# Last stage of a fused kernel: blocks read back in halves, a turn moved into the next tile, five weight loads held back

## The chip, the cores and the metric

The kernel runs on one core of a Trainium2 chip. The metric is the device time of one execution in microseconds, the median of three runs. The core's engines work side by side and wait for each other by semaphores: TensorE (PE, matmuls, with its weight loads as PEld), VectorE (DVE), ScalarE (ACT), GpSimd (POOL) and SyncE (SP), which here issues every DMA.

## The reference, cut to what matters

```
attn = softmax(scale * q_c @ k_c.T) @ v_c        # chunks of 64
x    = rmsnorm(attn) * rms_g
h    = silu(x @ w_gate) * (x @ w_val)            # 4608 x 1536
x2   = h @ w_out                                 # 4608 x 512
u    = x2 @ w_in                                 # 4608 x 2048
g    = u * cos(u)
out  = g @ w_out2                                # 4608 x 512
```

The last stage is the last line: 4608 tokens, 2048 inputs, 512 outputs, in f32. Each f32 operand is split into a high and a low part (`F32R`), and three matmuls stand for one.

## The kernel before

The kernel has four stages one after the other: attention with gate, value and silu; the product with `w_out`; the product with `w_in` and the cosine; and the last product, here the **last stage**. The last three multiply matrices in a Strassen-Winograd form, with seven products of half blocks in the place of eight. The last stage is the one the change is in.

The third stage writes g to DRAM (`gd`, three pieces of 1536 tokens). The last stage walks over NB = 6 tiles `s` of T = 768 tokens, in each over the seven products `j` in the order `PRODUCTS` = 1, 7, 6, 2, 5, 4, 3, and in each product over four groups `g` of 512 inputs. One step (s, j, g) is called a product here: 12 matmuls of 384 columns, `mm3` at L259. A tile has 28 of them.

For each tile and group, `fetch4` reads a block of g back as one SBUF tile `rawg` (128 partitions, 4 x 768 floats, 1.5 MB), in one DMA from the queue of SP (L815; in the first tile in six pieces, L992). The block has four quarters `b(r, c)`. `operand4` makes the operand of a product by `operand`: j = 1 takes b(0, 0) as it is; j = 7 writes b(1,1) - b(0,1) into `tmp` (L232); j = 6 changes b(0,1) and b(0,0) in place (L235, L236); j = 2, 5 and 3 take a quarter as it is; j = 4 subtracts b(0,0) from b(1,0) in place (L243). Then ACT casts the high part (L246) and DVE subtracts it for the low part (L247); both lie in a tile `xo`, of which the pool has five. Up to AHEAD = 5 operands are made ahead of the product that PE is at. `tmp` has one buffer, `rawg` four: one for each group. So a block for the next tile is asked for when the operand of j = 3 has been taken from the old one.

Sums are built up in PSUM. At the end of j = 1, 6 and 5 ACT copies the bank `b1` out (L982); DVE adds banks to it (L986); a finished quarter of the output is turned by DVE (`store`, a STREAM_TRANSPOSE at L974) and leaves by four DMAs (L978). The quarter of j = 3 is turned straight from the bank, after the last product of the tile.

Weights of the last stage lie in 28 places in SBUF, which the weights of the third stage (and the first six operands of the last stage) leave one by one in its last tile. `free` is called with a place as soon as the program has used it for the last time, and loads the next weight into it (L155).

The order of the instructions on each engine is not written out in this stage. A scheduler makes it from the program, the dependencies and its own estimate of times. Each engine then takes its instructions strictly in that order, PE's weight loads apart.

Of the kernel before, what the change touches and what calls it, by code (L numbers as in the profile page):

```python
# [9 lines left out]
F32 = mybir.dt.float32  # L10
# [10 lines left out]
P = 128  # L21
# [13 lines left out]
T = 768  # L35
H = T // 2
# [17 lines left out]

AHEAD = 5
EARLY4 = 6

BEHIND = 2

# [16 lines left out]
def kernel(  # L76
# [57 lines left out]
    last = [("out2", g, PLACE_A[j]) for j in PRODUCTS for g in range(N2 // 4)]  # L134
    wanted += last[:4] + [("op4", n, k) for n in range(EARLY4) for k in range(2)] + last[4:]
    place_of, weight, kept, early = {}, {}, {}, {}

    def free(*tags):
        for tag in tags:
# [77 lines left out]
    def blocks(raw):  # L217

        i = (slice(0, 2), slice(2, 4)), (slice(0, H), slice(H, T))
        return {(r, c): raw[:, i[0][r], i[1][c]] for r in range(2) for c in range(2)}  # L220
# [583 lines left out]
    G4 = N2 // 4  # L804
    raw4, ops4 = {}, {}

    def fetch4(s, g):
        if s < NB:
            t = rw.tile([P, 4, T], F32, tag="raw", name="rawg")
            raw4[s, g] = blocks(t)  # L810
            c = s * T % PIECE
            a = gd[s * T // PIECE][:, g, :, c : c + T]
            if s == 0:
                return t, a
            nc.sync.dma_start(out=t, in_=a)  # L815

    def operand4(s, j, g):
        n = made4[0]
        if n < EARLY4:
            tmp = third_p.tile([P, 2, H], F32, tag="tmp", name="tmp", bufs=1) if j == 7 else None  # L820
            to = [wp.tile([P, 2, H], F32R, tag=place_of["op4", n, k], name="xo") for k in range(2)]
            part = first4[g]
        else:
            tmp = tp.tile([P, 2, H], F32, tag="tmp", name="tmp") if j == 7 else None
            to = parts(xo_p)
            part = raw4[s, g]
        ops4[s, j, g] = operand(j, part, tmp, lambda: to)
        if j == PRODUCTS[-1]:
            fetch4(s + 1, g)

    first4 = {g: {} for g in range(G4)}

# [27 lines left out]
    with ExitStack() as st:  # L860
# [6 lines left out]
        def multiply(acc, s, j, g, first):  # L867
            w = weight["in", g, PLACE_A[j]]
            x = ops3[s, j]
            for p in range(2):  # L870
                mm3(
                    acc[:, p],
                    [(w[:, e, 0, p], w[:, e, 1, p], x[:, 0, e], x[:, 1, e]) for e in range(2)],
                    first,
                )
            if s == NB - 1:
                free(place_of["in", g, PLACE_A[j]])
            if g == G3 - 1 and j != 1:
                ahead3(made3[0] + 1)

# [75 lines left out]
    with ExitStack() as st:  # L956
# [29 lines left out]
            nc.vector.tensor_tensor(to, acc, to, op=ALU.add)  # L986
            return to

        tiles = [fetch4(0, g) for g in range(G4)]
        for g, cut in ((2, slice(H, T)), (3, slice(H, T)), (0, slice(0, T)), (1, slice(0, T)), (2, slice(0, H)), (3, slice(0, H))):  # L990
            t, a = tiles[g]
            nc.sync.dma_start(out=t[:, :, cut], in_=a[:, :, cut])  # L992
        z, xs = {}, {}
        for n, (s, j, g) in enumerate(seq4):
            bank = BANK[j]
            opens = j in (1, 2, 7, 4)
# [12 lines left out]
            product(z[bank], xs[g], g, j, opens and g == 0, slice(0, H))  # L1009
            if n < EARLY4:  # L1010
                free(*(place_of["op4", n, k] for k in range(2)))
            if g < G4 - 1:
                continue
            if j == 1:
                z[1] = saved(z["b1"], "s1")
            elif j == 6:
                z[6] = add(saved(z["b1"], "s6"), z["b3"])
            elif j == 5:
                store(s, 1, 1, add(saved(z["b1"], "s1"), z["b3"]), 0, H)
            elif j == 2:  # L1020
                store(s, 0, 0, add(z[1], z["b2"]), 0, H)
            elif j == 4:
                store(s, 1, 0, add(z[6], z["b4"]), 0, H)
            elif j == 3:
                store(s, 0, 1, z["b1"], 0, H)


# ---- launch: one core; inputs laid out for contiguous loads
# [47 lines left out]
```

## Time and profile before

| | us |
|---|---|
| median of three runs | 1713.21 (1713.1 to 1715.33) |
| the profiled execution | 1714.37 |
| its span, first to last instruction | 1712.2 |
| PE busy | 1663.2 (97%) |
| DVE busy | 1263.4 (74%) |
| ACT busy | 858.7 (50%) |
| mean granted TensorE clock | 0.991 |

PE is the bound nearly everywhere. A wait of PE is a hole in its row of the timeline; what ended it stands in brackets behind it. A group of matmuls in that row goes on as long as PE does not wait. One matmul in a long run takes about 0.174 us, but 0.44 us by itself, because its end is counted from issue to the last result.

### The profile page before, as it was taken

To read this page: it belongs to the slowest core of one execution; us is meant where nothing else is said; L and a number is where in the kernel's file an instruction comes from. 1 tells how busy PE (TensorE), PEld (TensorE's weight loads), DVE (VectorE), ACT (ScalarE), POOL (GpSimd) and SP (SyncE) were. 2 spreads that over 40 slices of the span, in tenths; PEclk is the share of its full clock that TensorE was granted. 3 is DMA by queue.
4 is the path that set the end of the run, shared out by engine and by line. 5 is a ranking of instruction groups with operands and counts; after the bars stand their busy time and mean duration, and the time that the engine had idled before them with its cause. 6 is when DMAs were issued, how large, how long until landed. Compare 5 with 4: busy or idle time off the path is not lost.

```text
span 1712.2 us, 27957 instructions
## 1 busy us (share of the span) xinstructions
PE 1663.2 (97%) x11016; PEld 1542.6 (90%) x11016; DVE 1263.4 (74%) x1831; ACT 858.7 (50%) x1242; POOL 63.0 (4%) x104
## 2 busy tenths in 40 slices
PE   6999999999999999999999999999998999999998
PEld 5988888888888888999999999999998889989988
DVE  7974578877877821777777788888886876876875
ACT  4643344554544421444444588888786433433432
POOL 2321000000000000000000000000000000000000
PEclk9999999999999999999999999999999999999999
DMA  8523587787888747633338733442459645045051
GB/s 324 184 78 111 159 246 222 246 254 238 243 242 236 213 157 254 210 140 138 141 145 271 270 118 135 148 142 104 147 200 354 239 165 185 17 169 182 12 175 38
DMA packets 273699, 310.38 MB, mean 181 GB/s; under 512 B 82592, under 2 KB 217248, under 8 KB 273568
## 3 DMA queue, kind: packets, MB, share of 16 engines
q1 hardware_dynamic: 273568, 308.60, 54.6%
q8 instruction: 87, 1.43, 0.4%
q14 instruction: 44, 0.36, 0.1%
HBM read 183.24 MB, written 125.30 MB: 180 GB/s over the span
## 4 chain that ended last, share of the span: by engine, by line
PE 84%; DMA 6%; DVE 5%; ACT 2%; issue 1%; SPq 0%; POOL 0%; ACTq 0%; DVEq 0%
PE b L259 46%; PE v L259 18%; PE g L259 17%; DMA rawg<-gd 5%; DVE xo L247 1%; PE o L450 1%; ACT xo L246 1%; PE sc L356 1%; PE tr L426 1%; PE pt L394 1%; DVE tmp L232 1%; DMA raw<-in_w_dram 1%; DVE rawg L236 1%; DMA rawx<-x2d 0%; DMA rawx<-gd 0%
## 5 line engine op out<-in xcount | busy, mean ns | idle before, releaser
L259 PE MATMUL b<-xo,w 128*128 128x384 f32 (+1 forms) x3576 | 632.8, 337 | 27.6 <-DVE xo L247 17.4
L259 PEld LDWEIGHTS b<-xo,w 128*128 128x128 f32 x3576 | 622.9, 190 | 37.5 <-DVE xo L247 21.3
L259 PE MATMUL b<-x,w 128*128 128x384 f32 x2016 | 352.1, 335 | 0.4 <-ACT z L886 0.2
L259 PEld LDWEIGHTS b<-x,w 128*128 128x128 f32 x2016 | 349.0, 188 | 3.4 <-ACT z L886 2.7
L259 PE MATMUL v<-xt,w 128*128 128x512 f32 (+1 forms) x1416 | 321.7, 377 | 0.0
L259 PE MATMUL g<-xt,w 128*128 128x512 f32 (+1 forms) x1416 | 314.6, 372 | 0.0
L259 PEld LDWEIGHTS g<-xt,w 128*128 128x128 f32 x1416 | 250.0, 188 | 45.8
L259 PEld LDWEIGHTS v<-xt,w 128*128 128x128 f32 x1416 | 248.3, 190 | 44.9
L246 ACT CAST xo<-rawg 128x768 fp32r<-128x768 f32 x140 | 114.7, 836 | 173.8 <-PE b L259 88.3
L499 ACT ACTIVATE sg<-g 128x512 f32<-128x512 f32 (+1 forms) x118 | 66.0, 560 | 227.2 <-PE g L259 218.4
L247 DVE TENSOR_TENSOR xo<-rawg,xo 128x768 fp32r<-128x768 f32 x140 | 131.1, 952 | 53.8 <-ACT xo L246 53.5
L503 DVE TENSOR_TENSOR h<-sg,v 128x512 f32<-128x512 f32 (+1 forms) x100 | 67.5, 678 | 117.0 <-PE v L259 96.2
L246 ACT CAST xo<-rawh 128x768 fp32r<-128x768 f32 x102 | 81.6, 835 | 95.8 <-DMA rawh<-hd 49.3
L247 DVE TENSOR_TENSOR xo<-rawh,xo 128x768 fp32r<-128x768 f32 x102 | 93.0, 954 | 36.7 <-ACT xo L246 36.7
L903 DVE SCALAR_TENSOR_TENSOR r<-r,u 128x768 f32<-128x768 f32 x72 | 68.6, 953 | 22.5 <-ACT r L902 22.4
L901 ACT ACTIVATE r<-r 128x768 f32<-128x768 f32 x72 | 60.8, 845 | 33.6 <-DVE r L900 33.4
L900 DVE SCALAR_TENSOR_TENSOR r<-r,u 128x768 f32<-128x768 int32 x72 | 68.6, 952 | 10.7 <-ACT r L899 10.7
L891 DVE TENSOR_TENSOR u<-b,z 128x768 f32<-128x768 f32 x72 | 68.5, 952 | 7.6 <-ACT z L886 6.4
L899 ACT CAST r<-u 128x768 int32<-128x768 f32 x72 | 59.7, 829 | 8.4 <-DVE u L891 8.2
L246 ACT CAST xo<-tmp 128x768 fp32r<-128x768 f32 x42 | 35.1, 835 | 53.2 <-DVE tmp L232 53.2
L902 ACT ACTIVATE r<-r 128x768 f32<-128x768 f32 x72 | 61.0, 847 | 1.2
L886 ACT COPY z<-b 128x768 f32<-128x768 f32 x72 | 56.4, 793 | 7.3 <-PE b L259 5.4
(101 smaller groups left out, 1435.0 us busy)
## 6 DMA issues: line engine op xcount, KB each, us to landing
gd<-r SPq DMA_DIRECT2D x96, 384.0 KB, 2.5
rawg<-gd SPq DMA_DIRECT2D x22, 1536.0 KB, 12.4
hd<-h SPq DMA_DIRECT2D x49, 512.0 KB, 4.8
kout<-wout SPq DMA_DIRECT2D x56, 448.0 KB, 4.7
w<-kout SPq DMA_DIRECT2D x49, 512.0 KB, 5.1
rawh<-hd SPq DMA_DIRECT2D x15, 1536.0 KB, 9.1
wraw<-in_w_dram SPq DMA_DIRECT2D x176, 128.0 KB, 3.0
qk<-in_qk_dram SPq DMA_DIRECT2D x36, 512.0 KB, 6.1
```

Source lines behind the costliest of these rows:

```text
L246: nc.scalar.copy(hi, a)
L247: nc.vector.tensor_tensor(lo, a, f32(hi), op=ALU.subtract)
L259: nc.tensor.matmul(acc, a, b, start=first and k == 0 and q == 0, stop=k == n - 1 and q == 2, skip_group_check=True)
L499: nc.scalar.activation(sg, g, AF.Silu)
L503: nc.vector.tensor_tensor(h, silu(acc[0]), acc[1], op=ALU.mult)
L886: nc.scalar.copy(t, acc)
L891: nc.vector.tensor_tensor(t, acc, part, op=ALU.add)
L899: nc.scalar.copy(k, u)
L900: nc.vector.scalar_tensor_tensor(q, k, -1.0, u, op0=ALU.mult, op1=ALU.add)
L901: nc.scalar.activation(q, q, AF.Sin, scale=math.pi)
L902: nc.scalar.activation(q, q, AF.Square, scale=math.sqrt(2 * PI2))
L903: nc.vector.scalar_tensor_tensor(q, q, -PI2, u, op0=ALU.add, op1=ALU.mult)
```

## The change

The block of a tile and group is no longer one tile of four quarter-columns of blocks but two halves, r = 0 with b(0,0) and b(0,1), and r = 1 with b(1,0) and b(1,1). Each half has four buffers of its own, so the space is the same. The half r = 0 of the next tile is asked for when the operand of j = 4 has been made, the half r = 1 when that of j = 3 has: the first half four products earlier than before. In the first tile 14 pieces are read in place of six, those that products 7 and 6 need first.

The turn of the quarter of j = 3 is written behind the second product of the next tile in place of the end of its own. Five of the places that the third stage's last group leaves are kept in a list, and their weights are asked for behind the first tile's blocks.

```diff
+HELD = (2, 7, 5, 4, 3)
...
-    def fetch4(s, g):
+    def fetch4(s, r, g):
         if s < NB:
-            t = rw.tile([P, 4, T], F32, tag="raw", name="rawg")
-            raw4[s, g] = blocks(t)
...
-            nc.sync.dma_start(out=t, in_=a)
+            t = rw.tile([P, 2, T], F32, tag=f"raw{r}", name="rawg")
+            raw4[s, g, r, 0], raw4[s, g, r, 1] = t[:, :, :H], t[:, :, H:]
+            if s:
+                load4(s, r, g, t, 0, T)
+            return t
+
+    def load4(s, r, g, t, lo, hi):
+        c = s * T % PIECE
+        nc.sync.dma_start(out=t[:, :, lo:hi], in_=gd[s * T // PIECE][:, g, 2 * r : 2 * r + 2, c + lo : c + hi])
...
-        if j == PRODUCTS[-1]:
-            fetch4(s + 1, g)
+        if j in (4, 3):
+            fetch4(s + 1, int(j == 3), g)
...
             if s == NB - 1:
-                free(place_of["in", g, PLACE_A[j]])
+                held.append(place_of["in", g, PLACE_A[j]])
+                if not (g == G3 - 1 and j in HELD):
+                    free(held.pop())
...
-        for g, cut in ((2, slice(H, T)), (3, slice(H, T)), (0, slice(0, T)), (1, slice(0, T)), (2, slice(0, H)), (3, slice(0, H))):
-            t, a = tiles[g]
-            nc.sync.dma_start(out=t[:, :, cut], in_=a[:, :, cut])
+        for g, r, lo, hi in (
+            [(g, r, H, T) for g in (2, 3) for r in range(2)]
+            + [(g, r, r * H, T) for g in (0, 1) for r in range(2)]
+            + [(g, 0, 0, H) for g in (2, 3)]
+            + [(g, 1, 0, H) for g in range(G4)]
+        ):
+            load4(0, r, g, both[g][r], lo, hi)
+        free(*held)
+        held.clear()
...
+            if late and g == 1:
+                store(*late.pop())
...
             elif j == 3:
-                store(s, 0, 1, z["b1"], 0, H)
+                late.append((s, 0, 1, z["b1"], 0, H))
```

How the scheduler now puts the instructions is seen at three places. Line numbers have moved by 3 to 7 (L247 is L250, L232 L235, L974 L981, L246 L249, L982 L989, L815 L820, L978 L985).

**DVE where the third tile takes over from the second.** Before, from the turn of j = 4 (`s_13836`) on; `b1_13636` is the second tile's bank, `rawg_13984`, `_14001`, `_14018` and `_14035` are the third tile's blocks:

```order
L974 STREAM_TRANSPOSE o_14050<-s_13836 128x2x12x32
L974 STREAM_TRANSPOSE o_14116<-b1_13636 128x2x12x32
L232 TENSOR_TENSOR tmp_14123<-rawg_13984 128x768
L247 TENSOR_TENSOR xo_14056<-rawg_13984,xo_14056 128x768
L235 TENSOR_TENSOR rawg_13984<-rawg_13984 128x2x384
L236 TENSOR_TENSOR rawg_13984<-rawg_13984 128x2x384
L247 TENSOR_TENSOR xo_14071<-rawg_14001,xo_14071 128x768
L247 TENSOR_TENSOR xo_14086<-rawg_14018,xo_14086 128x768
L247 TENSOR_TENSOR xo_14101<-rawg_14035,xo_14101 128x768
L247 TENSOR_TENSOR xo_14124<-tmp_14123,xo_14124 128x768
```

The same place now; `b1_13650` is the second tile's bank, `rawg_13931`, `_13949`, `_13967` and `_13985` the third tile's halves r = 0, `rawg_14012` the first half r = 1:

```order
L250 TENSOR_TENSOR xo_14084<-rawg_13931,xo_14084 128x768
L981 STREAM_TRANSPOSE o_14078<-s_13856 128x2x12x32
L250 TENSOR_TENSOR xo_14099<-rawg_13949,xo_14099 128x768
L250 TENSOR_TENSOR xo_14114<-rawg_13967,xo_14114 128x768
L250 TENSOR_TENSOR xo_14129<-rawg_13985,xo_14129 128x768
L981 STREAM_TRANSPOSE o_14179<-b1_13650 128x2x12x32
L235 TENSOR_TENSOR tmp_14145<-rawg_14012,rawg_13931 128x768
L238 TENSOR_TENSOR rawg_13931<-rawg_13931 128x2x384
L250 TENSOR_TENSOR xo_14146<-tmp_14145,xo_14146 128x768
L239 TENSOR_TENSOR rawg_13931<-rawg_14012,rawg_13931 128x2x384
```

The four low parts of the new tile's j = 1 stood behind the turn of the old tile's last bank and now stand ahead of it; the turn itself is still ahead of all of j = 7.

**ACT where the second tile takes over from the first.** Before; the `rawg` casts are those of j = 3 and of the new j = 1, `s<-b_13636` copies the second tile's sum of j = 1, the `tmp` casts are j = 7, and the `rawg` casts behind them are j = 6 and 2:

```order
L982 COPY s<-b_13136 128x768
L246 CAST xo<-rawg 128x768 x8
L246 CAST xo<-tmp 128x768 x2
L982 COPY s<-b_13636 128x768
L246 CAST xo<-tmp 128x768 x2
L246 CAST xo<-rawg 128x768 x8
```

Now, where `s<-b_13650` is that copy, and behind it the next boundary, where `s<-b_14144` is the third tile's:

```order
L249 CAST xo<-rawg 128x768 x8
L989 COPY s<-b_13650 128x768
L249 CAST xo<-tmp 128x768 x4
L249 CAST xo<-rawg 128x768 x8
L989 COPY s<-b_13650 128x768
L249 CAST xo<-rawg 128x768 x8
L249 CAST xo<-tmp 128x768 x2
L989 COPY s<-b_14144 128x768
L249 CAST xo<-tmp 128x768 x2
```

At this first boundary the copy now stands ahead of all four casts of j = 7; at the other four it stands between the second and the third, as before.

**SP in the second tile.** Before, with the stores of j = 2 and 5 (`o_13901`, `o_13974`) ahead and those of j = 4 and 3 behind:

```order
L978 DMA out_0_dram<-o_13901 32x12x64 x4
L978 DMA out_0_dram<-o_13974 32x12x64 x4
L815 DMA rawg_13984<-gd1_77 128x4x768
L815 DMA rawg_14001<-gd1_77 128x4x768
L815 DMA rawg_14018<-gd1_77 128x4x768
L815 DMA rawg_14035<-gd1_77 128x4x768
L978 DMA out_0_dram<-o_14050 32x12x64 x4
L978 DMA out_0_dram<-o_14116 32x12x64 x4
```

Now:

```order
L820 DMA rawg_13931<-gd1_77 128x2x768
L820 DMA rawg_13949<-gd1_77 128x2x768
L820 DMA rawg_13967<-gd1_77 128x2x768
L820 DMA rawg_13985<-gd1_77 128x2x768
L985 DMA out_0_dram<-o_13921 32x12x64 x4
L985 DMA out_0_dram<-o_14002 32x12x64 x4
L820 DMA rawg_14012<-gd1_77 128x2x768
L820 DMA rawg_14029<-gd1_77 128x2x768
L820 DMA rawg_14046<-gd1_77 128x2x768
L820 DMA rawg_14063<-gd1_77 128x2x768
L985 DMA out_0_dram<-o_14078 32x12x64 x4
L985 DMA out_0_dram<-o_14179 32x12x64 x4
```

The halves r = 0 stand ahead of the stores of j = 2 and 5, the halves r = 1 where the whole blocks stood.

## Rows read from the trace of the kernel before

**Rows 1.** The page: busy time, share of the span, instructions of each engine.

```profile
PE 1663.2 (97%) x11016; PEld 1542.6 (90%) x11016; DVE 1263.4 (74%) x1831; ACT 858.7 (50%) x1242; POOL 63.0 (4%) x104
```

**Rows 2.** Groups of instructions, 1309 to 1712 us: busy, mean ns | idle before, releasers.

```profile
L259 PE MATMUL b<-xo,w 128*128 128x384 f32 (+1 forms) x2064 | 370.5, 339 | 27.6 <-DVE xo L247 17.4 <-ACT xo L246 9.4 <-DVE o L974 0.7
...
L974 DVE STREAM_TRANSPOSE o<-b 128x768 f32<-128x768 f32 (+1 forms) x7 | 6.1, 869 | 40.8 <-PE b L259 40.8
```

**Rows 3.** Timeline of PE, last stage: start, us, instruction, count [idle before, releaser].

```profile
1343.53 35.73 PE L259 MATMUL b<-xo,w 128*128 128x384 f32 x204 [0.22 <-ACT xo L246]
1381.86 16.41 PE L259 MATMUL b<-xo,w 128*128 128x384 f32 x83 [2.61 <-DVE xo L247]
1398.75 0.44 PE L259 MATMUL b<-xo,w 128*128 128x384 f32 x1 [0.47 <-ACT xo L246]
1399.48 44.06 PE L259 MATMUL b<-xo,w 128*128 128x384 f32 x252 [0.29 <-ACT xo L246]
1446.15 14.18 PE L259 MATMUL b<-xo,w 128*128 128x384 f32 x71 [2.61 <-DVE xo L247]
...
1464.95 44.06 PE L259 MATMUL b<-xo,w 128*128 128x384 f32 x252 [0.29 <-ACT xo L246]
...
1529.86 44.06 PE L259 MATMUL b<-xo,w 128*128 128x384 f32 x252 [0.29 <-ACT xo L246]
...
1595.03 44.04 PE L259 MATMUL b<-xo,w 128*128 128x384 f32 x252 [0.30 <-ACT xo L246]
...
1660.36 40.89 PE L259 MATMUL b<-xo,w 128*128 128x384 f32 x251 [0.29 <-ACT xo L246]
```

**Rows 4.** Timeline of all engines, 1438 to 1470 us: the second boundary.

```profile
1443.41 0.98 DVE L974 STREAM_TRANSPOSE o<-b 128x768 f32<-128x768 f32 x1 [6.35 <-PE b L259]
1444.32 0.92 DVE L232 TENSOR_TENSOR tmp<-rawg 128x768 f32<-128x768 f32 x1
...
1445.15 0.95 DVE L247 TENSOR_TENSOR xo<-rawg,xo 128x768 fp32r<-128x768 f32 x1
...
1452.21 0.84 ACT L246 CAST xo<-rawg 128x768 fp32r<-128x768 f32 x1 [3.01 <-DMA rawg<-gd]
...
1454.94 0.96 DVE L232 TENSOR_TENSOR tmp<-rawg 128x768 f32<-128x768 f32 x1
...
1456.01 0.84 ACT L246 CAST xo<-tmp 128x768 fp32r<-128x768 f32 x1 [2.23 <-DVE tmp L232]
1456.76 0.79 ACT L982 COPY s<-b 128x768 f32<-128x768 f32 x1
1456.89 0.96 DVE L247 TENSOR_TENSOR xo<-tmp,xo 128x768 fp32r<-128x768 f32 x1
...
1458.63 0.95 DVE L232 TENSOR_TENSOR tmp<-rawg 128x768 f32<-128x768 f32 x1
```

**Rows 5.** Windows there: length, busy us (x) by engine, PEclk, DMA share, GB/s.

```profile
1440.00:1442.00 2.00, 2.00 (x14) 2.00 (x12) 0.00 (x0) 0.04 (x1) 0.00 (x0) 1.00 1.04 404
...
1446.00:1448.00 2.00, 1.84 (x7) 1.85 (x8) 1.97 (x4) 0.00 (x0) 0.00 (x0) 0.67 1.03 402
1448.00:1450.00 2.00, 2.00 (x8) 2.00 (x7) 1.60 (x2) 0.83 (x1) 0.00 (x0) 0.50 1.03 387
```

**Rows 6.** Timeline of SP, 1425 to 1450 us.

```profile
1432.34 3.57 SPq L815 DMA_DIRECT2D rawg<-gd  x4
```

**Rows 7.** L992, the first tile's block reads: duration ns, waits, time to landing.

```profile
L992 SPq DMA_DIRECT2D rawg<-gd x6: 411/975/3647, 1317.7 to 1322.7; - x6
...
  DVE rawg L235: 0.4, 2
...
DMA to landing us min/median/max: 6.5/13.0/15.7
```

**Rows 8.** Timeline of SP, 1316 to 1358 us: the first tile's reads, then ten weights.

```profile
1317.74 8.64 SPq L992 DMA_DIRECT2D rawg<-gd  x6
1326.48 14.82 SPq L155 DMA_DIRECT2D w<-kout  x10
```

More of the change, by code (lines that the diff above doesn't have):

```diff
@@ L136 @@
     place_of, weight, kept, early = {}, {}, {}, {}
+    held = []
     def free(*tags):
@@ L805 @@
     raw4, ops4 = {}, {}
-    def fetch4(s, g):
+    def fetch4(s, r, g):
         if s < NB:
-            t = rw.tile([P, 4, T], F32, tag="raw", name="rawg")
-            raw4[s, g] = blocks(t)
[L811 to L814, printed above, removed]
-            nc.sync.dma_start(out=t, in_=a)
+            t = rw.tile([P, 2, T], F32, tag=f"raw{r}", name="rawg")
[6 more added lines that the diff above has]
+        nc.sync.dma_start(out=t[:, :, lo:hi], in_=gd[s * T // PIECE][:, g, 2 * r : 2 * r + 2, c + lo : c + hi])
     def operand4(s, j, g):
@@ L825, in operand4 @@
             to = parts(xo_p)
-            part = raw4[s, g]
+            part = {(r, c): raw4[s, g, r, c] for r in range(2) for c in range(2)}
         ops4[s, j, g] = operand(j, part, tmp, lambda: to)
-        if j == PRODUCTS[-1]:
-            fetch4(s + 1, g)
+        if j in (4, 3):
+            fetch4(s + 1, int(j == 3), g)
     first4 = {g: {} for g in range(G4)}
@@ L987, in add @@
             return to
-        tiles = [fetch4(0, g) for g in range(G4)]
-        for g, cut in ((2, slice(H, T)), (3, slice(H, T)), (0, slice(0, T)), (1, slice(0, T)), (2, slice(0, H)), (3, slice(0, H))):
-            t, a = tiles[g]
-            nc.sync.dma_start(out=t[:, :, cut], in_=a[:, :, cut])
-        z, xs = {}, {}
+        both = [[fetch4(0, r, g) for r in range(2)] for g in range(G4)]
+        for g, r, lo, hi in (
[7 more added lines that the diff above has]
+        held.clear()
+        z, xs, late = {}, {}, []
         for n, (s, j, g) in enumerate(seq4):
```

## The prediction

> **What bounds the kernel now.** The engine line of the page comes first: PE is busy for 97% of the span [rows 1], so only PE's holes can be won, and what they drag behind them. The groups of the last stage say how large they are: 27.6 us idle ahead of its matmuls, 17.4 of it until a low part by DVE (L247) and 9.4 until a high part by ACT (L246); DVE in turn sits 40.8 us before the turns that it takes straight from a bank [rows 2]. PE's timeline says where. It runs without a hole for 204 or 252 matmuls, waits 2.61 us, runs seven products with halts, then runs for 252 again [rows 3]. That happens five times, where one tile takes over from the next; all five waits read 2.61.
>
> *What a boundary costs.* In a long run 252 matmuls take 44.06 us, of which some 0.27 is the drain of the last (one alone takes 0.44, one in a run 0.17), so a product of 12 takes 2.085 us and seven take 14.6. From the end of one long run to the start of the next, seven products lie, and it takes (start of the row less start and length of the one before) 20.2, 21.4, 20.9, 21.1 and 21.3 us [rows 3]. The five boundaries lose 5.6, 6.8, 6.2, 6.5 and 6.7 us: 31.8 us together, more than the waits add up to.
>
> *Why.* The all-engine timeline of the second boundary, where the old tile ends on PE at 1443.5 (I count from there as T), gives three reasons [rows 4]. First, the turn of the old bank can't begin before T, and DVE takes its work in order: turn, `tmp`, and only then the first low part of the new j = 1, at T + 1.6. PE waits out the three, 2.61 us, with the casts long possible. Second, the clock: after the gap the granted share is 0.67 and then 0.50 (1.2 in place of 2.4 GHz) in two windows of 2 us, with half the matmuls in them [rows 5]; 0.33 x 2 + 0.50 x 2 are 1.7 us of full pace lost. Third, blocks land late, the last at 1452.2, T + 8.7 [rows 4], so DVE comes late to j = 7 and 6, where it has four operations of 0.95 per group in 3.69 us (`tmp` to `tmp`, 1454.94 to 1458.63) against PE's 2.085; the rest of the loss, 1.3 to 2.5, is waits for it and their drains.
>
> **The change part by part.**
>
> *Two edits that move nothing.* Built without the held places, or with the turn written at the end of its own tile, the program has the same instructions in the same order, with the same waits and addresses on every engine: the scheduler had put both there anyway. The ten weights stand behind the block reads as before. I cost both at nothing, with no range.
>
> *The early half.* A half r = 0 may be asked for once j = 5's operand is made. With five `xo` buffers an operand waits for the end of the product five before it: for the last group of j = 5, the 20th product, that is the 15th of 28, at T - 13 x 2.085 = T - 27; cast and low part (0.84 + 0.95) give T - 25. Four of 0.79 MB at 403 GB/s [rows 5] take 7.8 us. Before, four blocks landed 19.9 us after the first issue at 1432.34 [rows 4, 6]; their 6.3 MB at that rate are 15.6, so 4.3 us come on top. The early halves land by T - 13, the first low part of j = 1 is wanted at T. The four low parts of j = 1 now stand ahead of the turn. Each follows its buffer: the last needs the product next to last but one, done at T - 2.1, and is ready by T - 0.2. PE's wait of 2.61 goes, and the clock's fall with it.
>
> *The late half.* It is issued where the whole blocks were, T - 11.2 [rows 6], behind the stores of j = 5. By the same 4.3 and 1.95 us each, the four land at T - 4.9, - 3.0, - 1.0 and + 0.9. DVE wants them for `tmp` at T + 0.8 and then every 3.69: no wait.
>
> *What is late next.* DVE's turn begins at T - 0.1, the first `tmp` at T + 0.8 [rows 4]. A low part of j = 7 begins 1.95 after its `tmp` (1454.94 to 1456.89), so the four end at T + 3.7, 7.4, 11.1 and 14.8. PE wants them at T + 8.3, 10.4, 12.5 and 14.6, the last two tenths later for the matmuls ahead of it. The cover is gone at the fourth: margin 0.1 us. ACT's copy of j = 1 waits for T + 8.3, and behind it the third cast is wanted at T + 9.2: margin 0.1 again (copy and next cast are 0.7 apart). I take 0.3 us for each of four boundaries, one drain: 1.2. Bounds: 0, and 1.2 each, 4.8 (the two waits with drains that the halts showed).
>
> *The first boundary gets a new wait.* There the copy stands ahead of all four casts of j = 7. The copy needs PE to be through j = 1, T + 8.3, and ACT takes its work in order, so the first cast begins at T + 9.1, and a second matmul (the first with the low part) can start 1.9 after that (1456.01 to the low part's end, 1457.84 [rows 4]), at T + 11.0. DVE sits at that low part, with the next three `tmp` behind it, which then follow every 3.69. The second matmuls of j = 7's four products start at T + 11.0, 14.7, 18.4 and 22.0; the last ends at T + 23.9 against 16.7 undisturbed. 7.2 us lost, against 5.6 before: 1.6 worse. Bounds: 5.6 (as before), and 8.9, if the clock's 1.7 falls wholly on top; I take none of it, since the next three products wait 1.6 us each for DVE, and a slow clock eats that first.
>
> *The start.* The first tile is read in 14 pieces in place of 6, of the same bytes. Groups 0 and 1 lack a quarter when j = 6 begins; 0.4 MB less ahead of it is about 1 us. DVE waited for those transfers 0.4 us in all [rows 7]; the rest of PE's wait there is DVE's own pace. Gain 0.4, which is also the upper bound. Ten pieces now stand ahead of j = 6 where six stood; should the four cost their median issue time of 0.975 us each [rows 7], the start loses 3.9: the lower bound.
>
> *A rule.* Blocks of 1.57 MB become 0.79 MB. The six pieces of the first tile are of both sizes, and the DMA engines' share in the windows at the boundary stands above 1 with transfers queued up [rows 5]: nothing idles between them, so I charge a byte no more than before. The Trainium skill speaks against the halves: "DMA: Bandwidth & Descriptors", section "Measured (HBM→SBUF, 128 partitions, SWDGE, issued from GpSimd)", asks for at least 1 MiB in a DMA, and the section "Anatomy of one DMA — SWDGE (gpsimd) path" gives a fixed 2.0 us for each. Were that cost paid one after the other, an estimate from that page is that the boundaries would still hide it and that the start would lose eight, less what DVE's own pace covers.
>
> *Sum.* Boundaries before 31.8, after 7.2 + 1.2 = 8.4: 23.4 gained; start 0.4: 23.8 us. Of the profiled execution, 1714.4 (span 1712.2, 2.2 around it), 1690.6 are left; of the median of 1713.2, which lies 1.2 below it, 1689.4.
>
> **The rivals.**
>
> *A wait is left at every boundary (12%).* The turn still stands ahead of all of j = 7, and DVE's chain has 0.1 us to spare. If `tmp`, the casts or the late halves run later than I count, each us goes to PE, with drains. At 2.5 us in each of four (the third reason above in full) the gain is 23.8 - 4 x 2.2 = 15: 1698. For it: DVE's 3.69 against 2.085. Against it: both halves land with 5 us and more to spare.
>
> *The first boundary clears as well (6%).* Were the copy not felt, its 7.2 would be 0.3, and the time 1682.5. The order of ACT speaks against it.
>
> *The change does not do what it says (4%).* The early halves stay behind something on SP until T, and the gap stays: 1713, within 0.2%. SP's new order has nothing ahead of them but stores of the tile before, so little speaks for it.
>
> *Slower (3%).* SP issues 14 reads ahead of ten weights, and the weights start only after the last. Six reads took 8.64 us to issue, 1.44 each, the longest 3.65 [rows 7, 8]. The first of the ten weights is used by product 18, at about 1343.5 + 7 x 2.085 = 1358 [rows 3], and lands up to 15.7 after its issue [rows 7]. So the reads may last until 1342.4, 24.7 us, 1.76 each; at 1.44 each it is 20.2, and PE doesn't notice. At 3.65 each it is 51 us, and PE stands 26 us, with the clock's fall 28: 28 - 23.8 = 4 slower, 1717.5. It decides from 3.3 us each.
>
> **How the numbers follow.** The forecast has 75%; its own bounds are first boundary 5.6 to 8.9, the others 0 to 4.8, start + 0.4 to - 3.9: with every term at its end, from 1686.6 to 1699. The rivals take the other 25%, and the range takes in most of the first of them: 1686 to 1698. About 0.2%, 3.4 us, is what a measurement here can tell from none. Faster by more: 75 + 12 + 6 = 93%; within: 4%; slower: 3%.
>
> **What would show it.** In the profile after, PE's timeline has no wait of 2.6 us at a tile's end and runs of more than 300 matmuls from the second boundary on; the turn of the bank by DVE still waits for PE, but the first low part of j = 1 is done by then. The granted clock is 1.00 through the last four boundaries. At the first, PE waits about 2.4 us after the new tile's four products of j = 1, and about 1.6 three times more, each until a cast and a low part from `tmp`, and ACT sits until PE at the copy. The late halves are all there before DVE asks. I would be wrong if the low part of j = 1 came behind the turn, if DVE or ACT waited for a read at a boundary, or if j = 7 kept PE waiting for us and not tenths.

## The result and the profile after

| | before | after |
|---|---|---|
| median of 4 runs each, us (after: 1686.75 to 1690.55) | 1714.01 | 1688.95 |
| ratio after / before, 95% interval | | 0.9852 [0.9835, 0.9869] |
| the profiled execution | 1714.37 | 1687.49 |
| its span | 1712.2 | 1685.7 |
| mean granted clock | 0.991 | 0.996 |

The changed kernel is 25.1 us faster. 1689.4 were predicted, and 1686 to 1698 as the range.

The engine line of the page after, to be laid beside [rows 1]: PE has lost 11.8 us of busy time with the same 11016 matmuls. Fewer matmuls run at the lower clock, and fewer stand alone with a long modelled end.

```profile
PE 1651.4 (98%) x11016; PEld 1535.1 (91%) x11016; DVE 1263.3 (75%) x1831; ACT 860.2 (51%) x1242; POOL 63.0 (4%) x104
```

The groups of the last stage, 1308 to 1686 us (busy, mean ns | idle before, releasers), beside [rows 2]: PE's idle ahead of its matmuls has gone from 27.6 to 12.9 us, and DVE's ahead of the turns from a bank from 40.8 to 10.3. The wait at `tmp` is the only one for a read that DVE has here.

```profile
L262 PE MATMUL b<-xo,w 128*128 128x384 f32 (+1 forms) x2064 | 359.3, 334 | 12.9 <-ACT xo L249 8.8 <-DVE xo L250 3.4 <-DVE o L981 0.7
...
L235 DVE TENSOR_TENSOR tmp<-rawg 128x768 f32<-128x768 f32 x22 | 20.8, 944 | 8.9 <-DMA rawg<-gd 8.9
...
L981 DVE STREAM_TRANSPOSE o<-b 128x768 f32<-128x768 f32 (+1 forms) x7 | 6.1, 869 | 10.3 <-PE b L262 9.6 <-DMA out_dram<-o 0.8
```

PE's timeline says where, beside [rows 3] (start, us, instruction, count, idle before and releaser). The stage starts with a wait of 4.83 us. The first boundary still has holes: 1.62 and 0.55, then twice a pair of 0.47 and 0.55, and 0.47 and 0.29. And then 1595 matmuls run without a hole, over four boundaries that each had a wait of 2.61 us and halts before.

```profile
1308.79 12.64 PE L262 MATMUL b<-xo,w 128*128 128x384 f32 x72
1326.26 0.69 PE L262 MATMUL b<-xo,w 128*128 128x384 f32 x1 [4.83 <-ACT xo L249]
...
1342.82 43.87 PE L262 MATMUL b<-xo,w 128*128 128x384 f32 x251 [0.16 <-ACT xo L249]
1388.31 0.45 PE L262 MATMUL b<-xo,w 128*128 128x384 f32 x1 [1.62 <-ACT xo L249]
1389.30 2.18 PE L262 MATMUL b<-xo,w 128*128 128x384 f32 x11 [0.55 <-DVE xo L250]
...
1392.95 2.18 PE L262 MATMUL b<-xo,w 128*128 128x384 f32 x11 [0.55 <-DVE xo L250]
...
1399.99 274.79 PE L262 MATMUL b<-xo,w 128*128 128x384 f32 x1595 [0.29 <-ACT xo L249]
```

*The second boundary*, beside [rows 4]. Of 1595 matmuls 251 belong to the old tile, at 0.174 us each, so T, the time at which the new tile's first matmul can start, is 1399.99 + 43.7 = 1443.7. (In the trace before this count gives 1399.48 + 43.7 = 1443.2; the prediction took 1443.5 there, with the drain of the last matmul in it. So its T is 0.3 later than the one used here.) In the timeline of all engines the turn of the old bank begins at T + 0.2; the low parts (`xo<-tmp,xo`) of j = 7 begin at 1446.72, 1450.40, 1454.06 and 1457.72. The fourth ends at 1458.68, T + 15.0. The old order put the turn and `tmp` ahead of j = 1; here nothing of j = 1 is left to do by then.

```profile
1443.92 0.98 DVE L981 STREAM_TRANSPOSE o<-b 128x768 f32<-128x768 f32 x1 [0.25 <-DMA out_dram<-o]
1444.83 0.92 DVE L235 TENSOR_TENSOR tmp<-rawg 128x768 f32<-128x768 f32 x1
...
1446.72 0.96 DVE L250 TENSOR_TENSOR xo<-tmp,xo 128x768 fp32r<-128x768 f32 x1
...
1457.72 0.96 DVE L250 TENSOR_TENSOR xo<-tmp,xo 128x768 fp32r<-128x768 f32 x1
```

The windows of that place (length, busy us and count by engine, granted clock, DMA share, GB/s), beside [rows 5]: the clock is at 1.00 where it was at 0.67 and 0.50, and the DMA engines are done with the reads by 1444 or so (49 GB/s in the next window), where before they were still at 387 GB/s from 1448 to 1450.

```profile
1442.00:1444.00 2.00, 2.00 (x13) 2.00 (x13) 1.04 (x2) 0.68 (x1) 0.00 (x0) 1.00 1.09 298
1444.00:1446.00 2.00, 2.00 (x14) 2.00 (x13) 1.97 (x3) 0.15 (x1) 0.00 (x0) 1.00 0.21 49
1446.00:1448.00 2.00, 2.00 (x13) 2.00 (x12) 2.00 (x3) 0.69 (x1) 0.00 (x0) 1.00 0.82 176
```

SP's timeline, beside [rows 6, 8]: the first tile's 14 pieces take 12.44 us to issue, the second boundary's early halves go out at 1413.59 (T - 30), the late ones at 1432.86 (T - 10.8), where the whole blocks went before.

```profile
1317.37 12.44 SPq L820 DMA_DIRECT2D rawg<-gd  x14
...
1413.59 5.51 SPq L820 DMA_DIRECT2D rawg<-gd  x4
...
1432.86 2.87 SPq L820 DMA_DIRECT2D rawg<-gd  x4
```

*The books of the two profiled executions.* I count from the start of one long run to that of the next, less 2.085 us for each product between (24 at the first boundary, 28 at the others). Before, the boundaries lose 5.9, 7.1, 6.5, 6.8 and 7.0: 33.3 us. After, the first loses 1399.99 - 1342.82 - 50.04 = 7.1, and the other four 0.1 each: 274.79 us less the last run of before, 40.89, for four tiles of 58.38. That is 7.5, so 25.8 are gained at boundaries. From the first row of the stage to its first long run it took 34.13 us and takes 34.03: 0.1. The stage begins 0.6 earlier, ahead of anything that the change touches. Together 26.5, as the spans differ.

### The profile page after: what moved, and what is told of

Read it like the earlier page. It is cut to its first block, busy times and chain, and to the rows that moved or that the text cites. A ratio compares the mean times of both kernels' runs of the same rounds, so it can differ in the third digit from the quotient of the medians.

```text
span 1685.7 us, 28029 instructions
## 1 busy us (share of the span) xinstructions
PE 1651.4 (98%) x11016; PEld 1535.1 (91%) x11016; DVE 1263.3 (75%) x1831; ACT 860.2 (51%) x1242; POOL 63.0 (4%) x104
## 4 chain that ended last, share of the span: by engine, by line
PE 95%; DVE 3%; ACT 1%; DMA 1%; issue 1%; SPq 0%; POOL 0%; ACTq 0%; DVEq 0%
PE b L262 56%; PE v L262 18%; PE g L262 17%; PE o L453 1%; PE sc L359 1%; PE tr L429 1%; PE pt L397 1%; ACT xo L249 0%; DMA rawg<-gd 0%; DMA raw<-in_w_dram 0%; DVE rawg L239 0%; DVE xo L250 0%; DVE p L390 0%; DVE tmp L235 0%; DVE z L387 0%
## 5 line engine op out<-in xcount | busy, mean ns | idle before, releaser
L262 PE MATMUL b<-xo,w 128*128 128x384 f32 (+1 forms) x3576 | 621.6, 334 | 12.9 <-ACT xo L249 8.8
L262 PEld LDWEIGHTS b<-xo,w 128*128 128x128 f32 x3576 | 615.5, 188 | 18.9 <-ACT xo L249 12.0
L249 ACT CAST xo<-rawg 128x768 fp32r<-128x768 f32 x140 | 114.8, 836 | 121.0 <-PE b L262 96.8
L250 DVE TENSOR_TENSOR xo<-rawg,xo 128x768 fp32r<-128x768 f32 x140 | 131.4, 953 | 51.6 <-ACT xo L249 51.3
L249 ACT CAST xo<-rawh 128x768 fp32r<-128x768 f32 x102 | 81.6, 835 | 95.6 <-DMA rawh<-hd 49.2
L250 DVE TENSOR_TENSOR xo<-rawh,xo 128x768 fp32r<-128x768 f32 x102 | 93.0, 954 | 36.1 <-ACT xo L249 36.1
L910 DVE SCALAR_TENSOR_TENSOR r<-r,u 128x768 f32<-128x768 f32 x72 | 68.6, 953 | 21.5 <-ACT r L909 21.4
L908 ACT ACTIVATE r<-r 128x768 f32<-128x768 f32 x72 | 60.8, 845 | 33.3 <-DVE r L907 32.9
L907 DVE SCALAR_TENSOR_TENSOR r<-r,u 128x768 f32<-128x768 int32 x72 | 68.6, 953 | 11.1 <-ACT r L906 11.0
L249 ACT CAST xo<-tmp 128x768 fp32r<-128x768 f32 x42 | 35.2, 837 | 63.2 <-DVE tmp L235 62.6
```

Source lines behind the costliest of these rows:

```text
L249: nc.scalar.copy(hi, a)
L250: nc.vector.tensor_tensor(lo, a, f32(hi), op=ALU.subtract)
L262: nc.tensor.matmul(acc, a, b, start=first and k == 0 and q == 0, stop=k == n - 1 and q == 2, skip_group_check=True)
L907: nc.vector.scalar_tensor_tensor(q, k, -1.0, u, op0=ALU.mult, op1=ALU.add)
L908: nc.scalar.activation(q, q, AF.Sin, scale=math.pi)
L910: nc.vector.scalar_tensor_tensor(q, q, -PI2, u, op0=ALU.add, op1=ALU.mult)
```

## The experiments

All are compared with the kernel before, run beside them on the same chip. Its median lay between 1713.9 and 1714.1 each time, so the times may also be laid beside each other. They stand together first.

| run | us, median | ratio to before, 95% |
|---|---|---|
| after | 1688.95 | 0.9852 [0.9835, 0.9869] |
| two_edits_out | 1687.7 | 0.985 [0.9835, 0.9864] |
| halves_late | 1685.49 | 0.984 [0.9823, 0.9856] |
| turn_behind | 1684.8 | 0.9831 [0.9816, 0.9846] |
| turn_first | 1702.26 | 0.9936 [0.9921, 0.9951] |
| act_in_order | 1681.56 | 0.9807 [0.9792, 0.9822] |
| held_behind | 1689.1 | 0.985 [0.9836, 0.9865] |
| both_ends | 1681.89 | 0.9812 [0.9795, 0.9828] |
| whole_low_first | 1751.56 | 1.0218 [1.0203, 1.0234] |
| asked_late | 1710.27 | 0.9979 [0.997, 0.9989] |

The theory has three parts: an early landing keeps DVE from making the new tile's first operands late; the four low parts of j = 1 then stand ahead of the turn, and PE's 2.61 us go; at the first boundary ACT's copy ahead of the casts of j = 7 is what still costs 7. The rivals put the gain down to the other two edits, to the split by itself or to the order by itself.

### Two of the three edits taken back

```diff
-HELD = (2, 7, 5, 4, 3)
+HELD = ()
...
-                late.append((s, 0, 1, z["b1"], 0, H))
+                store(s, 0, 1, z["b1"], 0, H)
```

> The changed kernel without the held places and with the turn of j = 3 written at the end of its own tile. My theory: the built program is the same row for row, so the time is that of the changed kernel, 1689 within its spread of 1686.8 to 1690.6. Rival: one of the two edits carries part of the gain; then the time is 1692 or more (the turn back ahead of the low parts would bring 2.6 us at each of five boundaries).

1687.7 us, with the same holes at the first boundary and one run of 1595 matmuls behind it. In the traces of the two kernels every engine takes the same instructions in the same order: the scheduler makes the same program with the two edits and without them. All of the change's effect is that of the halves, their buffers and their earlier request.

### Both halves asked for at j = 3

```diff
-        if j in (4, 3):
-            fetch4(s + 1, int(j == 3), g)
+        if j == 3:
+            fetch4(s + 1, 0, g)
+            fetch4(s + 1, 1, g)
```

> The changed kernel, but both halves of the next block are asked for when the operand of j = 3 has been made: the request is written four products later, the halves keep their own buffers. My theory: what wins is that half r = 0 has a buffer that comes free early; the scheduler issues its read as soon as it is, wherever it is written. The four later boundaries stay without a wait. At the first boundary two casts of j = 7 stand ahead of the copy again, so the 7.1 us lost there go: about 1682. Rival: the four products of lead are what wins; without them the low parts of j = 1 come behind the turn again, 1710 to 1714.

1685.49 us. For the question that it was made for it is half a miss: from the second boundary on the scheduler sends the early halves off as early as in the changed kernel, 19.3 us ahead of the late ones in both, whatever the place in the program. Only at the first boundary is the landing late, and there it shows, in the timeline of ACT: two casts of j = 1 wait for reads. The scheduler there put the last three low parts of j = 1 behind the turn again, and PE's timeline, below it, has one hole of 2.51 us and none after it. Where the changed kernel loses 7.1 us and none was expected, 4.4 are lost: 2.8 up to the end of the hole and 1.6 at the lower clock behind it (0.57 and 0.58 granted in two windows of 2 us).

```profile
1377.30 0.84 ACT L249 CAST xo<-rawg 128x768 fp32r<-128x768 f32 x1 [3.09 <-DMA rawg<-gd]
1381.20 0.83 ACT L249 CAST xo<-rawg 128x768 fp32r<-128x768 f32 x1 [3.07 <-DMA rawg<-gd]
```

PE's timeline at the same boundary and on to the end of the last long run:

```profile
1341.99 37.80 PE L262 MATMUL b<-xo,w 128*128 128x384 f32 x216 [0.19 <-ACT xo L249]
1382.30 288.82 PE L262 MATMUL b<-xo,w 128*128 128x384 f32 x1667 [2.51 <-DVE xo L250]
```

So the place of the request in the program is not what the change won by; that the early half has a buffer to go to is. What the early landing itself is worth needed SP's order by hand (the run asked_late, below).

### The turn behind the low parts, and ahead of them

Two kernels with the halves and with DVE and ACT in an order by hand through the stage. In the first the low parts of j = 1 stand ahead of the turn, and the copy behind the four casts of j = 7; j = 6's subtractions stand between those of j = 7.

```diff
+        with tc.manual_schedule(engines={ET.DVE, ET.Activation}):
...
-                late.append((s, 0, 1, z["b1"], 0, H))
+                store(s, 0, 1, z["b1"], 0, H)
```

The second differs from it in one thing: the four low parts of j = 1 wait until behind the turn.

```diff
-        nc.vector.tensor_tensor(lo, a, f32(hi), op=ALU.subtract)
+        if defer is not None:
+            defer.append((lo, a, f32(hi)))
+        else:
+            nc.vector.tensor_tensor(lo, a, f32(hi), op=ALU.subtract)
...
                     store(s, 0, 1, z["b1"], 0, H)
+                    for lo, a, hi in behind:
+                        nc.vector.tensor_tensor(lo, a, hi, op=ALU.subtract)
+                    behind.clear()
```

> The changed kernel's halves, with DVE and ACT in an order written out by hand in the last stage: low parts of j = 1, then the turn of the old bank, then j = 7 (with the two subtractions of j = 6 between), and ACT's copy of j = 1 behind all four casts of j = 7. My theory: no boundary loses anything, the first neither; the first tile may lose 1 to 2 us by the stiff order: 1682 to 1685. Rival: the wait at the first boundary has another cause than the copy (reads still under way there); then it stays, 1689. It is the base for the next kernel.

> As the kernel before it, with one thing moved: the four low parts of the new tile's j = 1 stand behind the turn of the old tile's last bank, as they did in the kernel before the change, while the halves are read as early as now. My theory (order on DVE): at each of five boundaries PE waits some 1.7 us for the first low part, and j = 7 comes 3.5 us later on DVE, 3 to 4 us in all, more if the clock falls: 15 to 22 us above the kernel before it, 1697 to 1706. Rival (late blocks were the cause of the old wait): with the blocks early the order doesn't matter, within 2 us of it.

1684.8 and 1702.26 us: 17.5 for the order alone, with halves and landing the same, 3.5 at each of five boundaries. Both rivals are out: the first kernel is not at 1689, and the second is not within 2 us of the first. In the traces the two differ only in the places of those low parts on DVE. PE's timeline of turn_behind has no hole of more than 0.2 us at any boundary; its first tiles:

```profile
1345.96 50.30 PE L267 MATMUL b<-xo,w 128*128 128x384 f32 x288 [0.30 <-ACT xo L252]
1396.42 58.54 PE L267 MATMUL b<-xo,w 128*128 128x384 f32 x336 [0.16 <-DVE xo L253]
```

PE's timeline of turn_first waits 1.74 us at all five, for the deferred low part (L1051), and at four of them again in j = 7:

```profile
1384.40 14.98 PE L270 MATMUL b<-xo,w 128*128 128x384 f32 x83 [1.74 <-DVE xo L1051]
1399.86 0.44 PE L270 MATMUL b<-xo,w 128*128 128x384 f32 x1 [0.47 <-ACT xo L252]
1400.85 43.98 PE L270 MATMUL b<-xo,w 128*128 128x384 f32 x252 [0.55 <-DVE xo L256]
1446.57 60.39 PE L270 MATMUL b<-xo,w 128*128 128x384 f32 x336 [1.74 <-DVE xo L1051]
1508.69 14.98 PE L270 MATMUL b<-xo,w 128*128 128x384 f32 x83 [1.74 <-DVE xo L1051]
```

Early landing without the order thus keeps 11.8 of the 29.3 us that turn_behind gains and gives up the rest. In both, the stiff order costs some 3 to 4 us in the first tile: 37.7 us from the stage's first row to the long run in turn_behind, against 34.0.

### The early request alone taken away

The kernel of turn_behind, with SP in program order too, so that eight halves go out in one block where the whole blocks did.

```diff
-        if j in (4, 3):
-            fetch4(s + 1, int(j == 3), g)
+        if j == 3:
+            if g == 0:
+                for k in range(G4):
+                    fetch4(s + 1, 0, k)
+            fetch4(s + 1, 1, g)
...
-        with tc.manual_schedule(engines={ET.DVE, ET.Activation}):
+        with tc.manual_schedule(engines={ET.DVE, ET.Activation, ET.SP}):
```

> The kernel of the run turn_behind, with halves, their own buffers and the same order by hand on VectorE and ScalarE, but with both halves of a tile asked for where the whole blocks were in the kernel before: eight reads in one block on SyncE, the four of r = 0 first. What is left out is the request four products earlier alone. By the issue at T - 11.2 and 1.95 us a half, the halves r = 0 land at T - 4.9 to T + 0.9 and the halves r = 1 at T + 2.8 to T + 8.7. My theory: the last low part of j = 1 is then done at T + 2.7, the turn at T + 3.7, and the low parts of j = 7 at T + 6.6, 10.3, 14.0 and 17.7, the fourth wanted at T + 14.6, so 3 to 4 us are lost at each of five boundaries, 15 to 19 over the 1684.8 of turn_behind: 1700 to 1704, with no wait at the tile's end and the waits in j = 7. The rival, that own buffers and the split are enough and the early request is worth nothing, gives 1684 to 1688; the other, that without the early request all is as with whole blocks, gives 1735 or more.

1710.27 us, 25.5 more than turn_behind, from which it differs in SP's order alone: neither rival (1684 to 1688, or 1735 and up), but 6 above my range. The place is the one that I named. PE has no hole at the tile's end and stands in j = 7; one tile takes 1463.97 - 1399.64 = 64.3 us in place of 58.7.

```profile
1399.64 52.77 PE L267 MATMUL b<-xo,w 128*128 128x384 f32 x300 [0.55 <-DVE xo L253]
...
1456.63 2.18 PE L267 MATMUL b<-xo,w 128*128 128x384 f32 x11 [0.55 <-DVE xo L253]
...
1463.97 54.66 PE L267 MATMUL b<-xo,w 128*128 128x384 f32 x311 [0.55 <-DVE xo L253]
```

The size is off since the reads went out at T - 7.7 (T is 1399.64 + 43.7 = 1443.3), some 3 us later than the whole blocks did, which went at T - 10.8 by the same count (T - 11.2 by the prediction's). In the timeline of all engines they stand right behind a store of the old tile. The first cast then waits 7.36 us for its half, the low parts of j = 1 follow, the turn begins at 1449.15 and ends at T + 6.8 in place of T + 3.7, and all of j = 7 comes behind it. So the 25.5 us pay for these 3 us too; with the reads at T - 10.8 it was not run. The order that wins with an early landing loses nearly all of its gain with a late landing: the turn now waits behind work whose data is not there.

```profile
1433.59 1.90 SPq L993 DMA_DIRECT2D out_dram<-o  x4
1435.59 6.76 SPq L825 DMA_DIRECT2D rawg<-gd  x8
...
1441.69 0.84 ACT L252 CAST xo<-rawg 128x768 fp32r<-128x768 f32 x1 [7.36 <-DMA rawg<-gd]
...
1449.15 0.98 DVE L989 STREAM_TRANSPOSE o<-b 128x768 f32<-128x768 f32 x1
```

### The order without the halves

The kernel before with whole blocks, and with turn_behind's order by hand.

```diff
+        with tc.manual_schedule(engines={ET.DVE, ET.Activation}):
...
+            if early6:
+                nc.vector.tensor_tensor(b(0, 1), b(0, 1), b(0, 0), op=ALU.subtract)
```

> The kernel before, blocks read whole into one pair of buffers, with the vector and scalar order by hand of turn_behind: the four low parts of a tile's second product ahead of the old tile's turn. If landing is what sets the boundary, the order alone is worth nothing and costs more, since the turn then stands behind subtractions whose block has not landed: 10 us lost at each boundary in place of 6.7, and 4 at the start, so 1730 to 1738. The rival, that the order of VectorE and ScalarE alone was the cause and the halves only happened to bring it, gives 1685 to 1690.

1751.56 us: 37.6 slower than before. The sign and the mechanism were as expected, the rival is out, and the size is 14 above the range, for the same reason as in asked_late: here too the reads went off later than before, right behind a store (1444.87, T - 7.7 with T at 1408.92 + 43.7 = 1452.6). In ACT's timeline the four casts of j = 1 wait for one block after the other, 3.9 us apart, the last until T + 12.1 instead of T + 9.0 (T + 8.7 by the prediction's count); a tile takes 1481.25 - 1408.92 = 72.3 us.

```profile
1452.99 0.83 ACT L249 CAST xo<-rawg 128x768 fp32r<-128x768 f32 x1 [9.39 <-DMA rawg<-gd]
1456.92 0.83 ACT L249 CAST xo<-rawg 128x768 fp32r<-128x768 f32 x1 [3.10 <-DMA rawg<-gd]
...
1464.69 0.83 ACT L249 CAST xo<-rawg 128x768 fp32r<-128x768 f32 x1 [3.02 <-DMA rawg<-gd]
```

PE's timeline, for T:

```profile
1408.92 43.80 PE L264 MATMUL b<-xo,w 128*128 128x384 f32 x251 [0.55 <-DVE xo L250]
```

With turn_first, turn_behind and the kernel before this makes a square. Late landing with the turn ahead: 1714 (the scheduler's order). Early landing with the turn ahead: 1702. Late landing with the turn behind: 1752. Early landing with the turn behind: 1685. The order is worth - 17.5 with the halves; without them it costs 38, in which the later reads and the stiff start have a part. Neither part alone is the change. Where the square says late, it has whole blocks. asked_late has halves, the same order on DVE and ACT and reads that leave at the same T - 7.7, and it takes 1710 in place of 1752. So of the 66.8 us between 1752 and 1685 41.3 belong to the split by itself, with which the four halves that j = 1 needs land ahead of the rest, and 25.5 to the early request (with SP's order by hand).

### The copy at the first boundary

The changed kernel, with ACT alone in program order in this stage.

```diff
+        with tc.manual_schedule(engines={ET.Activation}):
```

> The changed kernel with one difference: in the last stage's loop ScalarE takes its instructions in the order in which the program has them, so that at every boundary the four casts of the tile's second product go ahead of the old tile's last copy; VectorE's order is left as it was. My theory is that the 7.1 us that are still lost at the first boundary come from that copy standing ahead of casts that are ready: 1681 to 1683, the first boundary without a wait of over 1 us, the other four as before. The rival, that the first tile's second boundary is late for another reason (its early half lands late, or VectorE is behind), gives 1688 to 1690 and the same waits of 1.6 and 0.5 us in the same place.

1681.56 us, 7.4 less than after, and the rival's 1688 to 1690 is out. DVE's order is the same in both traces up to the last low part of j = 7 at this boundary. ACT's timeline has the copy behind the fourth cast, where it waits for nothing, as its first and last rows here show.

```profile
1378.69 0.84 ACT L249 CAST xo<-tmp 128x768 fp32r<-128x768 f32 x1 [3.18 <-DVE tmp L235]
...
1389.73 0.84 ACT L249 CAST xo<-tmp 128x768 fp32r<-128x768 f32 x1 [2.84 <-DVE tmp L235]
1390.47 0.80 ACT L989 COPY s<-b 128x768 f32<-128x768 f32 x1
```

PE's timeline has no hole of more than 0.2 us at any of the five boundaries; the first loses 0.4 us where it lost 7.1. The long run across it and the row behind it:

```profile
1341.16 50.30 PE L262 MATMUL b<-xo,w 128*128 128x384 f32 x288 [0.19 <-ACT xo L249]
1391.62 58.52 PE L262 MATMUL b<-xo,w 128*128 128x384 f32 x336 [0.16 <-DVE xo L250]
```

With both_ends, below, it is the fastest kernel here.

### The held weights really held back, and both ends at once

In the changed kernel the scheduler leaves the held loads where they were. Here SP alone takes its instructions in program order around the start of the stage.

```diff
+                if s == NB - 1 and g == G3 - 1:
+                    in_order = tc.manual_schedule(engines={ET.SP})
+                    in_order.__enter__()
...
+        in_order.__exit__(None, None, None)
```

> The changed kernel with one difference: around the start of the last stage SyncE takes its reads in program order, so that the five weight loads that the change meant to hold back do come behind the first tile's reads. My theory is that the reads then land some 4 us earlier, that the wait before the stage's second product falls from 4.8 to 1 to 2 us and that the clock stays up for more of the following 6 us: 3 to 4 us less, 1685. The rival, that the first reads are bound by the stores of the stage before and by their own issue, gives 1688 to 1690 with a wait of 4 us or more in the same place; a third way, the held weights landing too late for the first products that need them, shows as a wait on w and 1691 or more. The first boundary is as in the changed kernel, 7.1 us lost.

1689.1 us, the same as after: the theory's 1685 is out, and the rival has the time and the wait. Fourteen weight loads stand behind the reads in place of ten. PE's first wait is 4.11 in place of 4.83 us, and 33.6 us pass from the stage's first row to the long run, in place of 34.0; the wait of `tmp` for the first reads is 8.1 in place of 8.9. So half a us at most is seen of the held loads, and that is less than two executions of one program differ by: two_edits_out, which is the same program as after, took 35.2 us from the stage's first row to the long run. The reads are bound by something else: in both kernels they start to go out at 1317.3 or 1317.4, right behind the third stage's last store and two weight loads. Whether they could go earlier was not tried.

```profile
1325.77 0.69 PE L262 MATMUL b<-xo,w 128*128 128x384 f32 x1 [4.11 <-ACT xo L249]
```

The last kernel puts turn_behind's order, from the first tile's 17th product on, together with this.

> The order by hand of the run turn_behind, but only from product 16 of the first tile on, and the weight loads held back as in held_behind. My theory adds up what the two give by themselves: 7 us from the first boundary, 0 to 4 from the start, so 1677 to 1682. If the two do not add up (the held weights collide with the reads of the second tile), 1683 to 1688.

1681.89 us, at the upper end of the range: 7 from the boundary, nothing from the start. It doesn't differ from act_in_order. In its PE timeline the whole stage behind the start is one run.

```profile
1341.31 325.81 PE L267 MATMUL b<-xo,w 128*128 128x384 f32 x1883 [0.42 <-DVE xo L253]
```

## Why the prediction was right, point by point

*Two edits at nothing.* Right: two_edits_out.

*The boundaries before, 31.8.* Too small by 1.5. The term went by the ends of long runs and left out the drain of the last matmul, some 0.27 to 0.3 at each of five; by starts of rows they lose 33.3.

*The early half.* Right in what it does: the four reads were issued from T - 30 to T - 25, the last where the prediction has its last group, all reads were done by about T + 0.5, the low parts of j = 1 done before the turn, the 2.61 gone and the clock's fall with it. asked_late shows what the early request is worth: 25.5 us, with the 3 us of later reads in it.

*The late half.* Right: issued at T - 10.8, which is T - 11.1 by the prediction's count (11.2 there), and no wait for it.

*The margin at j = 7, 0.3 for each of four boundaries.* The mechanism was placed well, and the size was a little high: the fourth low part ended at T + 15.0, which is T + 14.7 in the prediction's count (14.8 by my chain), and PE's row shows no hole; 0.1 was lost at each. The margin of 0.1 that the prediction states is none by its own figures: ready at 14.8, wanted at 14.6 and two tenths. The first of the rivals, a wait left at every boundary, had the right place too, since asked_late and turn_first stop there; it fell because both halves land in time.

*The first boundary, 7.2.* Right, with its reason: 7.1 measured, and act_in_order gets back 6.7 of it. The second matmuls of j = 7's products were put at T + 11.0, 14.7, 18.4 and 22.0. By the prediction's count T is 1378.5, and they start at T + 10.8 (1389.30), 14.4 and 18.1, with the fourth at T + 21.5. The copy and what it holds up read so in the timeline of all engines:

```profile
1386.73 0.80 ACT L989 COPY s<-b 128x768 f32<-128x768 f32 x1 [9.57 <-PE b L262]
1387.42 0.83 ACT L249 CAST xo<-tmp 128x768 fp32r<-128x768 f32 x1
1388.29 0.96 DVE L250 TENSOR_TENSOR xo<-tmp,xo 128x768 fp32r<-128x768 f32 x1 [7.07 <-ACT xo L249]
```

The granted clock was 1.00 here, so that the bound of 8.9, with the clock's fall on top, did not come in.

*The start, 0.4.* 0.1, and no run tells so little from none: the same program took 34.0 in one profiled execution and 35.2 in another (two_edits_out). The reads were to be there sooner for j = 6, and DVE's 0.4 us of waits for them are gone; but its wait for the read of the first `tmp`, ahead of anything that the order among the pieces could bring, is 8.9 us where it was 8.2. The rival that turned slower by the issue of 14 reads needed 3.3 us each; they took 0.89.

*The rule on the size of a transfer.* The Trainium skill, "DMA: Bandwidth & Descriptors", section "Measured (HBM→SBUF, 128 partitions, SWDGE, issued from GpSimd)", wants 1 MiB or more in a DMA. It speaks of transfers issued from GpSimd; here SyncE issues them. The halves are 0.79 MB, and the trace does not bear out a price here: the windows at the boundary stand at 394 to 411 GB/s, as before. The fixed 2.0 us for each that the same page of the Trainium skill gives in its section "Anatomy of one DMA — SWDGE (gpsimd) path", paid eight times more at the start, would be 16 us there as an estimate from it; the start took 34.03 against 34.13.

*Sum.* 25.8 + 0.1 for the stage in place of 23.4 + 0.4. The 2.1 more are the drains (1.5), the four boundaries (0.8) and the first (0.1), less 0.3 at the start. Between the two profiled executions, 26.9 us apart, the forecast of 23.8 was 3.1 short; the other 1.0 are the 0.6 by which the stage began earlier and 0.4 outside the spans. It came out 0.45 from the median partly by luck: the runs after lie in the median 1.5 above the one that was profiled, and the forecast started from the median of the first three runs of before, 0.8 below that of all.

## What to carry to other kernels

Where one buffer per block is refilled at the end of a tile, ask which part of the block is dead first, and give that part buffers of its own. At four of five boundaries the scheduler here then moved the request by itself, and with the landing the order changed. A data-ready order and an early landing belong together: the early landing alone brought 12 of 29 us, and the order alone, with whole blocks, cost 38. Put work ahead of a release that needs data which is not there, and it costs more than the wait that it removes. Then read each in-order engine at each boundary apart: one copy in the wrong place at one of five boundaries cost some 7 us, more than a quarter of what the whole change won.

## What the runs showed of the hardware

*The clock's fall after a gap can be free.* In turn_first the same gap of 1.74 us stands at all five boundaries. At the second the granted share fell to 0.50 (1.2 GHz) and 0.65 in two windows behind it; at the first, as at the other three, it stayed at 1.00 (2.4 GHz).

```profile
1386.00:1388.00 2.00, 2.00 (x14) 2.00 (x13) 1.97 (x4) 0.07 (x1) 0.00 (x0) 1.00 1.00 221
1388.00:1390.00 2.00, 2.00 (x13) 2.00 (x12) 2.00 (x3) 0.77 (x1) 0.00 (x0) 1.00 0.13 27
...
1448.00:1450.00 2.00, 2.00 (x8) 2.00 (x7) 1.98 (x3) 0.00 (x0) 0.00 (x0) 0.50 0.58 131
1450.00:1452.00 2.00, 2.00 (x9) 2.00 (x9) 1.98 (x3) 0.83 (x1) 0.00 (x0) 0.65 0.41 89
```

In the kernel before, the clock fell behind the 2.61 us at all five boundaries: in the windows of 1 us at 1383, 1447, 1512, 1577 and 1642 it stood at 0.50.

The tile with the fall in turn_first took 1508.69 - 1446.57 = 62.1 us, those without 62.2 (1446.57 - 1384.40): DVE's pace in j = 7 set the end either way, and PE's row, with 336 matmuls and no hole, lacks the 0.47 and 0.55 that it waits in j = 7 elsewhere: the slow clock took their place. That the same gap of 1.74 us does it at one place and not at another fits the Trainium skill, "TensorE: Matmul & The Clock Gate", section "What's actually happening", by which the gate looks at the engine's activity on a beat of its own, which the kernel does not start.
